# Attention and two gated MLPs on one core: eight weight units split earlier, high halves on VectorE, small operations on GpSimd

## The chip, the cores and the metric

The kernel runs on one core of one Trainium2 chip. Times are microseconds (us) of device time for one execution. The engines are called by the profile's names: PE is TensorE's matmul stream and PEld its weight loads, DVE is VectorE, ACT is ScalarE, POOL is GpSimd, and SP is SyncE, which here only issues DMAs.

## The reference

Attention of 4 batches with 12 heads over 448 tokens and 64 features, then two MLPs over the 1792 tokens. Cut to what matters:

```python
def rmsnorm(x, g):
    rms = np.sqrt(np.mean(x * x, axis=-1, keepdims=True) + 1e-06)
    return x / rms * g
q_n, k_n = (rmsnorm(q, g_q), rmsnorm(k, g_k))
scores = scale * np.matmul(q_n, k_n.transpose(0, 1, 3, 2))
scores = scores - np.max(scores, axis=-1, keepdims=True)
attn = np.exp(scores)
attn = attn / (np.sum(attn, axis=-1, keepdims=True) + 1e-09)
attn_out = np.matmul(attn, v)
x = attn_out.transpose(0, 2, 1, 3).reshape(B * S, H * D)      # 1792 x 768
x = (x @ w_a) * (x @ w_b) @ w_out                             # d_ff 1536, no activation
h = x @ w_in                                                  # d_ff 2048
g = np.maximum(h, 0.0) + alpha * np.minimum(h, 0.0)
out = g @ w_out2                                              # 1792 x 768
```

Queries, keys, values and norm weights are float32. The weight matrices of the MLPs are float64, so each value arrives as eight bytes.

## The kernel before

**Two programs in one.** The attention runs in steps (`att_steps`, 84 with work, each on two tiles of 128 query rows; a pair of heads has seven tiles): scores, softmax, transposition of the probabilities, product with the values. The 24 pairs of heads, six in a batch, follow each other. The six of batch 0 come first, in float32 with transposes on PE ("the first attention", up to 118 us). The others use float16 in two halves, high and low, and transposes by DMA. The MLPs run in 16 stages, `a0 y0 h0 o0 a1 y1 a2 h1 o1 y2 a3 h2 y3 o2 h3 o3`: the letter says which matrix is multiplied (a: `w_a` and `w_b`; y: `w_out`; h: `w2_in`; o: `w2_out`), the digit which batch. Attention steps of batches 1 to 3 are handed out among the ticks of a stage. `RATE` says how many a stage gets, and what is still missing before an a stage is run ahead of it.

**Weights.** Each matrix is read in units, 128x768 for a, y and h, 128x512 for o, 76 in all (a 24, y 12, h 16, o 24). The first time a unit is needed it is made on the chip, in four steps:

- `w_load`: SP's queue brings the float64 words, three buffers (`raw_p`).
- `w_convert`: ACT shifts the exponent of the upper words (L631), DVE shifts (L634) and joins the lower bits (L637) into a float32 tile. For o units DVE then multiplies by `inv_h`, the inverse scale of each of the rows' h units (L643). ACT sums the squares (L653).
- `w_scale`: PE sums over the partitions (`total`), and `power` makes from this a scale and its inverse, both powers of two.
- `w_split`: ACT writes the float16 high half (L686), DVE the low half (L687), and a DMA stores both in scratch memory (L690). The next batch reloads them from there, in `w_load`.

`advance(u)` drives these: while unit u is in use, loads run 10 units ahead, conversions 8, scales 6, splits 3. In the first attention it is called at every second step and reaches `u = -1`, which is what is ready when stage a0 begins. The products of PE take three matmuls for each tile (`prod`): high by high, high by low, low by high.

**Order.** A framework with a scheduler sets a fixed order of the instructions of each engine when the program is built, and waits are by semaphores. Each engine and each queue takes its instructions in that order.

**Small steps that the change touches.** `prep1` computes the inverse roots of the norms by three Newton rounds on a 128x30 tile on DVE, for two head pairs at a time; `prep2` multiplies queries and keys by them. `soft` takes the row maximum (DVE, L414), scales it by `esc` (ACT, L427, batches 1 to 3) and takes the exponential (ACT, L431) with its sum `su`. `probs_f` and `probs` add 1e-9 to `su` (DVE, L441 and L467) and take the reciprocal. In stage h the result of PE goes through ACT and DVE to a float32 tile, which is split by `cg` into `G` (L741, L742). In stage o each 128 columns are transposed back on PE and scaled by `cum` on DVE (L856) into `ob` for the output. The pool `slot` holds 35 tiles of 128x448 words for X, AB, Y and G.

Of the kernel before, what the change touches and what calls it, by code (L numbers as in the profile page):

```python
# [19 lines left out]
def attention_gated_mlps_kernel(  # L20
# [73 lines left out]
    icg = const.tile([128, 1], F32, name="icg")  # L94
    ssv = const.tile([KP, B, NP], F32, name="ssv")
# [14 lines left out]
    def power(total, s, i):  # L110
# [10 lines left out]
        nc.vector.tensor_scalar(i.bitcast(I32), h, 1.0, float(49 << 23), op0=ALU.mult, op1=ALU.add)  # L121
# [59 lines left out]
    def setup4():  # L181
# [10 lines left out]
        nc.vector.tensor_scalar(al, al, -1.0, 1.0, op0=ALU.mult, op1=ALU.add)  # L192
        nc.vector.tensor_scalar(icg, icg, 2.0 ** 31, None, op0=ALU.mult)
# [49 lines left out]
    def prep1(gs, c0=0, c1=NS):  # L243
# [166 lines left out]
    def soft(m):  # L410
# [15 lines left out]
        else:  # L426
            nc.scalar.activation(out=nm, in_=nm, func=AF.Copy, scale=esc)  # L427
# [33 lines left out]
    def probs(m):  # L461
# [5 lines left out]
        nc.vector.tensor_scalar(su, su, 1e-9, 2.0 ** -14, op0=ALU.add, op1=ALU.mult)  # L467
# [61 lines left out]
    state = dict(pin=True)  # L529
# [71 lines left out]

    def size(kind):
        return CHAINS[kind][2] * 128

    def w_load(u):
# [3 lines left out]
        if key in scratch:  # L609
            t = wh_p.tile([128, 2, 768], F16, tag="w16", name="w16")[:, :, 0:n]  # L610
            nc.sync.dma_start(out=t, in_=scratch[key])
            w16[u] = t
            return
# [7 lines left out]
    def w_convert(u):  # L621
# [18 lines left out]
        if kind == "o":  # L640
            k = CHAINS["o"][2]
            t3 = t.rearrange("p (k f) -> p k f", f=128)
            nc.vector.tensor_tensor(  # L643
                t3, t3,
                inv["h"][:, part * k:(part + 1) * k].unsqueeze(2).to_broadcast([128, k, 128]),
                op=ALU.mult,
            )
# [13 lines left out]
    def w_scale(u):  # L661
# [10 lines left out]
        for x in us:  # L672
            scales[x] = sc[:, (x - us[0]) // parts:(x - us[0]) // parts + 1]

# [5 lines left out]
    def w_split(u):  # L680
# [4 lines left out]
        w = wh_p.tile([128, 2, 768], F16, tag="w16", name="w16")[:, :, 0:n]  # L685
# [280 lines left out]
```

## Time and profile before

| what | value |
|---|---|
| median of 3 runs | 1285.5 us (1284.17 to 2438.65) |
| profiled execution, own time | 1286.1 us |
| span of the profiled execution | 1283.9 us |
| PE busy | 1177.9 us (92%) |
| PEld busy | 604.0 us (47%) |
| DVE busy | 709.6 us (55%) |
| ACT busy | 734.5 us (57%) |
| POOL busy | 9.8 us (1%) |
| mean granted clock of PE | 0.968 |
| moved by DMA | 234.66 MB, mean 183 GB/s |

A busy time is the time in which the engine had an instruction in work, over the whole span; weight loads overlap matmuls. The span runs from the first to the last recorded instruction, so 2.2 us of the execution's own time lie around it. The shares are means over stages that differ: the second half holds little but matmuls and reloads, the first half holds the attention and all the making of weights.

The stages begin, by their first matmul, at 118 (a0), 232 (y0), 295 (h0), 363 (o0) and 466 us (a1); y1 begins at 655 us.

### The profile page before, as it was taken

The page shows a single profiled execution, that of the slowest core. Times are in us where ns is not written, and L with a number is a line of the kernel's source. Part 1 is how long each engine was busy: PE and PEld are TensorE (multiplying, and loading weights), DVE is VectorE, ACT ScalarE, POOL GpSimd, SP SyncE. Part 2 cuts the span into 40 slices and gives each one's busy share as a digit, 9 for nine tenths or more (in the row PEclk, how much of TensorE's full clock was granted, in tenths as well). Part 3 has the DMA queues.
Part 4 walks back from the last instruction along what each step waited for, and adds up shares of the span by engine and source line. Part 5 has one row for each costly group of instructions (what it writes and reads, how often), then busy time and mean ns, then how long its engine had stood idle before and what let it go on. Part 6 is the DMA issues. An engine that isn't in the chain of part 4 may idle for free. (4 is left out here: it accounts for less than half of the span.)

```text
span 1283.9 us, 18197 instructions
## 1 busy us (share of the span) xinstructions
PE 1177.9 (92%) x6574; PEld 604.0 (47%) x6574; DVE 709.6 (55%) x1500; ACT 734.5 (57%) x1480; POOL 9.8 (1%) x32
## 2 busy tenths in 40 slices
PE   6897998888888889887999989999999999999998
PEld 3454544444443444443545545555555555555554
DVE  7988788879897857576545166443111351102410
ACT  7999898999886867577554256544222342212310
POOL 1000000000000000000000000000000000000000
PEclk9998998898998999997999999999999999999999
DMA  6548999999989899986865375687533333344343
GB/s 187 157 156 195 299 295 299 268 296 269 285 220 251 238 235 226 206 210 164 204 153 152 115 169 133 153 189 179 150 112 113 121 112 119 94 137 137 104 124 86
DMA packets 324489, 234.66 MB, mean 183 GB/s; under 512 B 190992, under 2 KB 297744, under 8 KB 324400
## 3 DMA queue, kind: packets, MB, share of 16 engines
q1 hardware_dynamic: 324288, 233.43, 68.9%
q8 instruction: 52, 0.85, 0.3%
q0 software_dynamic: 112, 0.07, 0.1%
q14 instruction: 37, 0.30, 0.1%
HBM read 155.79 MB, written 32.24 MB: 146 GB/s over the span
## 5 line engine op out<-in xcount | busy, mean ns | idle before, releaser
L108 PEld LDWEIGHTS <-w 128*128 128x128 f16 x4896 | 480.2, 100 | 488.8 <-issue 55.5
L108 PE MATMUL p<-x,w 128*128 128x448 f16 x1728 | 339.7, 356 | 10.1 <-ACT t L760 6.7
L108 PE MATMUL p<-g,w 128*128 128x448 f16 x1152 | 232.9, 359 | 9.9 <-DVE w L687 6.9
L108 PE MATMUL p<-y,w 128*128 128x448 f16 x1152 | 225.2, 357 | 0.0
L108 PE MATMUL p<-ab,w 128*128 128x448 f16 x864 | 170.8, 359 | 1.9 <-ACT ab L741 1.9
L108 PE MATMUL s<-kT,qT 128*64 128x448 f16 (+1 forms) x588 | 105.5, 408 | 32.4 <-ACT pf L431 24.7
L414 DVE TENSOR_REDUCE nm<-s 128x2 f32<-128x896 f32 x84 | 91.0, 1084 | 36.2 <-PE s L108 35.9
L475 DVE SCALAR_TENSOR_TENSOR p<-pf,ri,p 128x448 f16<-128x448 f32 x126 | 83.2, 680 | 37.9 <-ACT p L474 37.9
L474 ACT ACTIVATE p<-pf,ri 128x448 f16<-128x448 f32 x126 | 79.9, 662 | 31.9 <-DMA pT<-p 23.5
L431 ACT ACTIVATE pf<-s,nm,esc 128x448 f32<-128x448 f32 x126 | 90.2, 720 | 2.9 <-DVE p L475 1.5
L763 DVE SCALAR_TENSOR_TENSOR ab<-p,inv_a,t 128x448 f32<-128x448 f32 x48 | 32.6, 679 | 100.2 <-PE p L108 99.8
L847 ACT ACTIVATE t<-p,inv_o 128x448 f32<-128x448 f32 x24 | 25.6, 1066 | 102.2 <-PE p L108 102.2
L631 ACT ACTIVATE wf<-raw 128x768 f32<-128x768 f32 (+1 forms) x76 | 63.2, 835 | 28.7 <-DMA raw<-in_moe_w_out_dram 8.8
L856 DVE TENSOR_SCALAR ob<-p,cum 112x512 f32<-112x512 f32 x24 | 18.0, 749 | 107.1 <-PE p L854 56.8
L687 DVE SCALAR_TENSOR_TENSOR w<-wf,sc,w 128x768 f16<-128x768 f32 (+1 forms) x76 | 69.8, 927 | 4.0 <-ACT w L686 3.7
L766 ACT ACTIVATE junk<-ab 128x448 bf16<-128x448 f32 x48 | 27.5, 573 | 74.9 <-DVE ab L763 74.1
L833 DVE SCALAR_TENSOR_TENSOR t<-t,al,p 128x448 f32<-128x448 f32 x64 | 43.4, 679 | 47.6 <-ACT t L832 47.6
L637 DVE SCALAR_TENSOR_TENSOR wf<-raw,wf 128x768 int32<-128x768 int32 (+1 forms) x76 | 65.8, 868 | 0.4
L832 ACT ACTIVATE t<-p 128x448 f32<-128x448 f32 x64 | 34.6, 541 | 54.3 <-PE p L108 54.1
L686 ACT ACTIVATE w<-wf,sc 128x768 f16<-128x768 f32 (+1 forms) x76 | 64.5, 862 | 0.3 <-DVE sc L118 0.3
L653 ACT ACTIVATE junk<-wf 128x768 bf16<-128x768 f32 (+1 forms) x76 | 59.0, 776 | 8.5 <-DVE wf L643 2.9
L741 ACT ACTIVATE g<-t,cg 128x448 f16<-128x448 f32 x64 | 42.6, 666 | 34.7 <-DVE t L833 34.6
(131 smaller groups left out, 1003.3 us busy)
## 6 DMA issues: line engine op xcount, KB each, us to landing
w<-sc_a SPq DMA_DIRECT2D x72, 384.0 KB, 3.2
w<-sc_h SPq DMA_DIRECT2D x48, 384.0 KB, 3.1
w<-sc_o SPq DMA_DIRECT2D x72, 256.0 KB, 3.1
w<-sc_y SPq DMA_DIRECT2D x36, 384.0 KB, 3.2
raw<-in_moe_w_in_dram SPq DMA_DIRECT2D x16, 768.0 KB, 7.0
raw<-in_moe_w_out_dram SPq DMA_DIRECT2D x24, 512.0 KB, 5.0
raw<-in_moe_w_a_dram SPq DMA_DIRECT2D x12, 768.0 KB, 7.2
raw<-in_moe_w_b_dram SPq DMA_DIRECT2D x12, 768.0 KB, 6.0
```

Source lines behind the costliest of these rows:

```text
L108: nc.tensor.matmul(out=o, lhsT=a, rhs=b, start=first, stop=last)
L414: nc.vector.tensor_reduce(out=nm, in_=ps[:, :, 0:S], axis=AX.X, op=ALU.max, negate=True)
L431: nc.scalar.activation(out=pf, in_=ps[:, j, 0:S], func=AF.Exp, bias=nm[:, j:j + 1], scale=scale[j], accum_out=su[:, j:j + 1],)
L474: nc.scalar.activation(out=t[:, 0, :, 0:KP], in_=pf, func=AF.Copy, scale=r)
L475: nc.vector.scalar_tensor_tensor(out=t[:, 1, :, 0:KP], in0=pf, scalar=r, in1=t[:, 0, :, 0:KP], op0=ALU.mult, op1=ALU.subtract,)
L631: nc.scalar.activation(out=t, in_=hi.bitcast(F32), func=AF.Prelu, scale=2.0 ** -112, alpha=-(2.0 ** 32))
L637: nc.vector.scalar_tensor_tensor(out=ti, in0=lo, scalar=29, in1=ti, op0=ALU.logical_shift_right, op1=ALU.bitwise_or)
L653: nc.scalar.activation(out=junk(768, size(kind)), in_=t, func=AF.Square, accum_out=sums[0][:, j:j + 1])
L686: nc.scalar.activation(out=w[:, 0], in_=t, func=AF.Copy, scale=s)
L687: nc.vector.scalar_tensor_tensor(out=w[:, 1], in0=t, scalar=s, in1=w[:, 0], op0=ALU.mult, op1=ALU.subtract)
L741: nc.scalar.activation(out=x[:, 0], in_=t, func=AF.Copy, scale=s)
L833: nc.vector.scalar_tensor_tensor(out=t, in0=t, scalar=al[:, f:f + 1], in1=ps, op0=ALU.mult, op1=ALU.add)
```

## The change

**Units.** `EARLY` = 8 units get their halves in 16 tiles of the `slot` pool, and `advance` may run up to unit `LEAD` = 5 in the first attention, at three calls in four steps; in a0 it waits until the unit in use passes 5. For odd units the high half is made by DVE, for even ones by ACT as before. The scratch write is two DMAs instead of one.

**inv_h.** The multiplication of the o units by `inv_h` is taken out. `h_scales` folds it into the scale of `G` (`cgf`), once the last h unit has its scale. Until then stage h0 keeps `G` tiles as float32 in slots, and splits two in each later tick.

**Small operations.** To POOL go: the inverse power of two in `power`, the Newton rounds (from pair 3 on, four operations a round where there were three), the scaling of the maximum by `esc`, the addition to `su`, and two operations of the setup. `ob` goes from DVE to ACT. `RATE` gives a0 six attention steps for four, and o0 six for eight.

```diff
@@ power @@
-        nc.vector.tensor_scalar(i.bitcast(I32), h, 1.0, float(49 << 23), op0=ALU.mult, op1=ALU.add)
+        nc.gpsimd.tensor_scalar(i.bitcast(I32), h, 1.0, float(49 << 23), op0=ALU.mult, op1=ALU.add)
...
+        eng = nc.vector if gs[0] < 3 else nc.gpsimd
         for _ in range(3):
-            nc.vector.tensor_tensor(t, r, r, op=ALU.mult)
-            nc.vector.scalar_tensor_tensor(
-                out=t, in0=t, scalar=-0.5, in1=m, op0=ALU.mult, op1=ALU.mult
-            )
-            nc.vector.scalar_tensor_tensor(
-                out=r, in0=t, scalar=1.5, in1=r, op0=ALU.add, op1=ALU.mult
-            )
+            eng.tensor_tensor(t, r, r, op=ALU.mult)
+            eng.tensor_tensor(t, t, m, op=ALU.mult)
+            eng.tensor_scalar(t, t, -0.5, 1.5, op0=ALU.mult, op1=ALU.add)
+            eng.tensor_tensor(r, r, t, op=ALU.mult)
...
-            nc.scalar.activation(out=nm, in_=nm, func=AF.Copy, scale=esc)
+            nc.gpsimd.tensor_scalar(nm, nm, esc, 1.0, op0=ALU.mult, op1=ALU.mult)
...
-        nc.vector.tensor_scalar(su, su, 1e-9, None, op0=ALU.add)
+        nc.gpsimd.tensor_scalar(su, su, 1e-9, 1.0, op0=ALU.add, op1=ALU.mult)
...
+    EARLY, LEAD = 8, 5
+    early_w = [[slot(f"w{u}_{l}") for l in range(2)] for u in range(EARLY)]
...
-        if kind == "o":
-            k = CHAINS["o"][2]
-            t3 = t.rearrange("p (k f) -> p k f", f=128)
-            nc.vector.tensor_tensor(
...
+        if (kind, n) == ("h", KF2 - 1):
+            h_scales()
+
+    def h_scales():
+
+        mx = sm_p.tile([128, 1], F32, tag="mh", name="mh")
+        ci = sm_p.tile([128, 1], F32, tag="mh", name="ci")
+        nc.vector.tensor_reduce(out=mx, in_=inv["h"], axis=AX.X, op=ALU.max)
+        nc.vector.tensor_scalar(
+            ci.bitcast(I32), mx.bitcast(I32), -1.0, float(254 << 23), op0=ALU.mult, op1=ALU.add
+        )
+        nc.vector.tensor_scalar(cgf, inv["h"], ci, cg, op0=ALU.mult, op1=ALU.mult)
+        nc.gpsimd.tensor_tensor(icg, icg, mx, op=ALU.mult)
+        state["cgf"] = True
...
-        nc.scalar.activation(out=w[:, 0], in_=t, func=AF.Copy, scale=s)
+        if u < EARLY:
+            w = [x.rearrange("p l s -> p (l s)")[:, 0:n] for x in early_w[u]]
...
+        if u % 2:
+            nc.vector.tensor_scalar(w[0], t, s, None, op0=ALU.mult)
+        else:
+            nc.scalar.activation(out=w[0], in_=t, func=AF.Copy, scale=s)
...
-        nc.sync.dma_start(out=scratch[stream[u]], in_=w)
+        for l in range(2):
+            nc.sync.dma_start(out=scratch[stream[u]][:, l], in_=w[l])
...
-        advance(u)
+        advance(max(u, LEAD))
...
-            G[b, f] = split(t, cg, f"g{b}_{f}")
+            if state["cgf"]:
+                for x in sorted({f, min(raw)}):
+                    one(x)
+        for x in sorted(raw):
+            one(x)
...
-            nc.vector.tensor_scalar(ob, po, cum[:PT, b:b + 1], None, op0=ALU.mult)
+            nc.scalar.activation(out=ob, in_=po, func=AF.Copy, scale=cum[:PT, b:b + 1])
...
-    RATE = {"a0": 4, "y0": 5, "h0": 4, "o0": 8, "a1": 14, "y1": 7, "a2": 4, "h1": 4, "o1": 8, "y2": 6}
+    RATE = {"a0": 6, "y0": 5, "h0": 4, "o0": 6, "a1": 14, "y1": 7, "a2": 4, "h1": 4, "o1": 8, "y2": 6}
...
-        W0, EVERY = 4, 2
+        W0 = 3
...
-            if n >= W0 and (n - W0) % EVERY == 0:
-                advance((n - W0) // EVERY - 9 if n < 22 else -1)
+            if n >= W0:
+                advance(min((n - W0) * 3 // 4 - 9, LEAD))
```

In the order of ACT, at the first head pair's output in the first attention, there stood before (`wf<-raw` is the first step of a conversion, `junk` the sum of squares, `pf` an exponential, `pT<-p` and `kT` copies of transposes, `x<-x,sx` that output):

```order
L431 ACTIVATE pf,su<-s,nm,r 128x448 x2
L368 ACTIVATE sq,ssv<-vn 112x512
L631 ACTIVATE wf<-raw 128x768 x2
L459 COPY pT<-p 112x4x128
L523 ACTIVATE x_0_560<-x,sx 128x448
L368 ACTIVATE sq,ssv<-vn 112x512
L322 COPY kT_107<-p 128x448
L459 COPY pT<-p 112x4x128 x2
L431 ACTIVATE pf,su<-s,nm,r 128x448 x2
L653 ACTIVATE junk,ss<-wf 128x768
```

In the changed program the same engine has, around the same output:

```order
L633 ACTIVATE wf<-raw 128x768
L430 ACTIVATE pf,su<-s,nm,r 128x448 x2
L367 ACTIVATE sq,ssv<-vn 112x512
L647 ACTIVATE junk,ss<-wf 128x768
L458 COPY pT<-p 112x4x128
L522 ACTIVATE x_0_599<-x,sx 128x448
L633 ACTIVATE wf<-raw 128x768 x2
L367 ACTIVATE sq,ssv<-vn 112x512
L647 ACTIVATE junk,ss<-wf 128x768
L633 ACTIVATE wf<-raw 128x768
L321 COPY kT_107<-p 128x448
```

Conversions stand closer together: by the end of the first attention ACT has 15 for 11 and 14 sums of squares for 9, and DVE has 9 low halves for 5 and 4 high halves where it had none.

At the start of stage o0, DVE had before (`wf` are o units in conversion, `w` their halves, `g` a split of stage h):

```order
L634 TENSOR_SCALAR wf<-wf 128x512
L687 SCALAR_TENSOR_TENSOR w_4155<-wf,sc,w_4155 128x512
L637 SCALAR_TENSOR_TENSOR wf<-raw,wf 128x512
L833 SCALAR_TENSOR_TENSOR t<-t,al,p 128x448
L643 TENSOR_TENSOR wf<-wf,inv_h 128x512
L634 TENSOR_SCALAR wf<-wf 128x512
L742 SCALAR_TENSOR_TENSOR g_15_4162<-t,cg,g_15_4162 128x448
L637 SCALAR_TENSOR_TENSOR wf<-raw,wf 128x512
L687 SCALAR_TENSOR_TENSOR w_4189<-wf,sc,w_4189 128x512
L643 TENSOR_TENSOR wf<-wf,inv_h 128x512
```

In the changed program DVE has in that stage, after the start value of a Newton chain (`r<-t`, L260):

```order
L699 TENSOR_SCALAR w_4442<-wf,sc 128x512
L260 TENSOR_SCALAR r<-t 128x30
L382 SCALAR_TENSOR_TENSOR v_4491<-vr,sx,v_4491 112x8x64
L702 SCALAR_TENSOR_TENSOR w_4416<-wf,sc,w_4416 128x512
L702 SCALAR_TENSOR_TENSOR w_4442<-wf,sc,w_4442 128x512
L327 TENSOR_TENSOR qr<-qr,r 128x448
L636 TENSOR_SCALAR wf<-wf 128x512
L330 TENSOR_TENSOR qr<-qr,gbc 128x448
L639 SCALAR_TENSOR_TENSOR wf<-raw,wf 128x512
```

The products with `inv_h` are gone, a high half (L699) has come, and the user of the chain's result (`qr<-qr,r`) stands three instructions behind its start value, while the rounds between the two stand on POOL.

On POOL the program before has, from the end of the setup on (`cum` is the output's scale, first computed at the end of stage y0):

```order
L160 DMA gbc<-in_g_q_dram 128x64
L151 TENSOR_SCALAR gT<-gT 128x1
L161 DMA gkb<-in_g_k_dram 128x64
L162 DMA al<-in_moe_alpha_dram 128x16x1
L813 TENSOR_TENSOR cum<-ix,iab 128x1
L814 TENSOR_TENSOR cum<-cum,iy 128x1
```

In the changed program POOL has inside the first attention, among others (`su` feeds the reciprocal of a softmax, `inv_a` the a units' inverse scales, `t` and `r` are a Newton round):

```order
L440 TENSOR_SCALAR su<-su 128x2 x2
L122 TENSOR_SCALAR inv_a<-pw 128x2
L440 TENSOR_SCALAR su<-su 128x2
L122 TENSOR_SCALAR inv_a<-pw 128x2
L263 TENSOR_TENSOR t<-r 128x30
L264 TENSOR_TENSOR t<-t,m 128x30
L265 TENSOR_SCALAR t<-t 128x30
L266 TENSOR_TENSOR r<-r,t 128x30
```

Between the setup and the first `cum` POOL had nothing; now a whole Newton chain of twelve operations stands between two `su`. Over the program POOL has 30 Newton rounds in ten chains, 84 `su`, 63 `nm` and 45 inverse powers.

## Rows read from the trace of the kernel before

**Rows 1.** Busy time of each engine by stage; last: clock, DMA share, GB/s.

```profile
0.00:118.00 118.00, 91.56 (x554) 53.48 (x555) 99.52 (x302) 104.04 (x230) 5.68 (x16) 0.94 0.62 167
118.00:226.00 108.00, 99.06 (x543) 49.90 (x542) 89.95 (x176) 95.33 (x187) 0.00 (x0) 0.97 1.05 292
226.00:295.00 69.00, 55.85 (x308) 28.20 (x308) 58.59 (x122) 63.84 (x123) 1.79 (x4) 0.90 1.06 279
295.00:363.00 68.00, 63.54 (x342) 32.28 (x341) 62.34 (x125) 57.93 (x110) 0.00 (x0) 0.95 0.97 276
363.00:466.00 103.00, 84.50 (x465) 39.61 (x463) 89.30 (x197) 80.70 (x173) 0.00 (x0) 0.93 0.92 236
466.00:598.00 132.00, 111.35 (x665) 54.48 (x664) 84.58 (x180) 83.22 (x189) 0.19 (x1) 0.95 0.91 212
...
655.00:1284.00 629.00, 617.82 (x3398) 319.17 (x3396) 189.32 (x326) 211.02 (x396) 2.10 (x11) 0.99 0.49 131
```

**Rows 2.** The same view, two stretches inside the first attention.

```profile
32.00:64.00 32.00, 26.48 (x176) 15.46 (x173) 29.57 (x100) 31.86 (x73) 0.00 (x0) 0.98 0.56 157
64.00:96.00 32.00, 29.62 (x183) 16.65 (x181) 26.03 (x63) 29.63 (x67) 0.00 (x0) 0.96 0.50 156
```

**Rows 3.** Waits of PE: us in total, times, longest us.

```profile
PE s L108 <- ACT pf L431: 24.7, 12, 4.8
...
PE p L108 <- DVE w L687: 6.9, 5, 2.2
```

**Rows 4.** Groups of ACT from 0 to 118 us: busy us, mean ns.

```profile
L631 ACT ACTIVATE wf<-raw 128x768 f32<-128x768 f32 x9 | 8.4, 945 | 0.0
L653 ACT ACTIVATE junk<-wf 128x768 bf16<-128x768 f32 x9 | 7.9, 878 | 0.0
```

**Rows 5.** Groups of DVE by shape, whole span.

```profile
L687 DVE SCALAR_TENSOR_TENSOR w<-wf,sc,w 128x768 f16<-128x768 f32 x52 | 52.2, 1011 | 3.7 <-ACT w L686 3.7
L637 DVE SCALAR_TENSOR_TENSOR wf<-raw,wf 128x768 int32<-128x768 int32 x52 | 49.5, 954 | 0.4
...
L634 DVE TENSOR_SCALAR wf<-wf 128x768 int32<-128x768 int32 x52 | 28.8, 556 | 23.2 <-ACT wf L631 22.8
...
L634 DVE TENSOR_SCALAR wf<-wf 128x512 int32<-128x512 int32 x24 | 10.1, 421 | 4.5 <-ACT wf L631 4.2
L262 DVE SCALAR_TENSOR_TENSOR t<-t,m 128x30 f32<-128x30 f32 x33 | 6.2, 188 | 0.6
...
L441 DVE TENSOR_SCALAR su<-su 128x2 f32<-128x2 f32 x21 | 3.4, 163 | 3.3 <-ACT pf L431 3.2
```

**Rows 6.** Groups of ACT by shape, whole span.

```profile
L686 ACT ACTIVATE w<-wf,sc 128x768 f16<-128x768 f32 x52 | 48.0, 932 | 0.0
...
L427 ACT ACTIVATE nm<-nm,esc 128x2 f32<-128x2 f32 x63 | 18.4, 292 | 46.9 <-DVE nm L414 46.9
L686 ACT ACTIVATE w<-wf,sc 128x512 f16<-128x512 f32 x24 | 16.5, 710 | 0.3 <-DVE sc L118 0.3
```

**Rows 7.** Groups of DVE from 363 to 466 us.

```profile
L643 DVE TENSOR_TENSOR wf<-wf,inv_h 128x512 f32<-128x512 f32 x18 | 12.2, 683 | 0.0
...
L856 DVE TENSOR_SCALAR ob<-p,cum 112x512 f32<-112x512 f32 x5 | 3.7, 746 | 0.1
```

**Rows 8.** Timeline of POOL: start us, us, instruction [idle before].

```profile
230.47 0.95 POOL L813 TENSOR_TENSOR cum<-ix,iab 128x1 f32<-128x1 f32 x1 [221.20 <-DVE pw L115]
...
293.55 0.19 POOL L815 TENSOR_TENSOR cum<-cum,icg 128x1 f32<-128x1 f32 x1
293.82 0.19 POOL L816 TENSOR_TENSOR cum<-cum,ix 128x1 f32<-128x1 f32 x1
```

**Rows 9.** Timeline of DVE beside the first of them.

```profile
230.36 1.01 DVE L687 SCALAR_TENSOR_TENSOR w<-wf,sc,w 128x768 f16<-128x768 f32 x1
```

**Rows 10.** DMA issues from 466 to 598 us: count, KB each, us to landing.

```profile
w<-sc_a SPq DMA_DIRECT2D x21, 384.0 KB, 4.6
...
pT<-p SPq DMA_TRANSPOSE x32, 3.5
```

More of the change, by code (lines that the diff above doesn't have):

```diff
@@ L94, in attention_gated_mlps_kernel @@
     icg = const.tile([128, 1], F32, name="icg")
+    cgf = const.tile([128, KF2], F32, name="cgf")
     ssv = const.tile([KP, B, NP], F32, name="ssv")
@@ L191, in setup4 @@
         nc.vector.tensor_scalar(cg, cg, 2.0 ** -31, None, op0=ALU.mult)
-        nc.vector.tensor_scalar(al, al, -1.0, 1.0, op0=ALU.mult, op1=ALU.add)
-        nc.vector.tensor_scalar(icg, icg, 2.0 ** 31, None, op0=ALU.mult)
+        nc.gpsimd.tensor_scalar(al, al, -1.0, 1.0, op0=ALU.mult, op1=ALU.add)
+        nc.gpsimd.tensor_scalar(icg, icg, 2.0 ** 31, None, op0=ALU.mult)
     P = [dict() for _ in range(B * NP)]
@@ L527, in pv_out @@
         P[g] = None
-    state = dict(pin=True)
+    state = dict(pin=True, cgf=False)
     preps = (prep2, prep3, prep4)
@@ L611, in w_load @@
             nc.sync.dma_start(out=t, in_=scratch[key])
-            w16[u] = t
+            w16[u] = [t[:, l] for l in range(2)]
             return
@@ L684, in w_split @@
         n = t.shape[1]
-        w = wh_p.tile([128, 2, 768], F16, tag="w16", name="w16")[:, :, 0:n]
-        nc.scalar.activation(out=w[:, 0], in_=t, func=AF.Copy, scale=s)
+        if u < EARLY:
+            w = [x.rearrange("p l s -> p (l s)")[:, 0:n] for x in early_w[u]]
+        else:
+            w = wh_p.tile([128, 2, 768], F16, tag="w16", name="w16")[:, :, 0:n]
+            w = [w[:, l] for l in range(2)]
+        if u % 2:
+            nc.vector.tensor_scalar(w[0], t, s, None, op0=ALU.mult)
+        else:
+            nc.scalar.activation(out=w[0], in_=t, func=AF.Copy, scale=s)
         nc.vector.scalar_tensor_tensor(
-            out=w[:, 1], in0=t, scalar=s, in1=w[:, 0], op0=ALU.mult, op1=ALU.subtract
+            out=w[1], in0=t, scalar=s, in1=w[0], op0=ALU.mult, op1=ALU.subtract
         )
-        nc.sync.dma_start(out=scratch[stream[u]], in_=w)
+        for l in range(2):
+            nc.sync.dma_start(out=scratch[stream[u]][:, l], in_=w[l])
         w16[u] = w
@@ L723, in unit @@
     def unit():
-        w = w16[cur[0]]
-        return w.rearrange("p l (k f) -> p l k f", f=128)
+        return [x.rearrange("p (k f) -> p k f", f=128) for x in w16[cur[0]]]
     def prod(o, w, kk, x, first, last):
-        hi, lo = w[:, 0, kk, :], w[:, 1, kk, :]
+        hi, lo = w[0][:, kk, :], w[1][:, kk, :]
         mm(o, hi, x[:, 0], first, False)
@@ L823, in stage_h, with one @@
     def stage_h(b):
+        raw = {}
+        def one(f):
+            t = raw.pop(f)
+            G[b, f] = x = slot(f"g{b}_{f}")
+            nc.scalar.activation(out=x[:, 0], in_=t, func=AF.Copy, scale=cgf[:, f:f + 1])
+            nc.vector.scalar_tensor_tensor(
+                out=x[:, 1], in0=t, scalar=cgf[:, f:f + 1], in1=x[:, 0],
+                op0=ALU.mult, op1=ALU.subtract,
+            )
         for f in range(KF2):
@@ L830, in stage_h @@
             next_w()
-            t = tmp()
+            raw[f] = t = tmp() if state["cgf"] else slot32(f"g32_{b}_{f}")
             nc.scalar.activation(out=t, in_=ps, func=AF.Relu, scale=-1.0)
@@ L860, in finish @@
             )
+        c = cum[:, b:b + 1]
+        nc.gpsimd.tensor_tensor(c, ix[:, b:b + 1], iab[:, b:b + 1], op=ALU.mult)
+        nc.gpsimd.tensor_tensor(c, c, iy[:, b:b + 1], op=ALU.mult)
+        nc.gpsimd.tensor_tensor(c, c, icg, op=ALU.mult)
+        nc.gpsimd.tensor_tensor(c, c, ix[:, b:b + 1], op=ALU.mult)
         late = None
@@ L915, in attention_gated_mlps_kernel @@
         state["pin"] = False
-        advance(-1)
+        advance(LEAD)
         def step():
```

11 lines of the change are left out of this document (1 added, 10 removed).

## The prediction, made before the changed kernel had run

> **What bounds the kernel now.** I read the stages first, because the shares over the whole span mix two halves that differ. In the view of busy time by stage [rows 1] the reader should subtract PE's busy time from each stretch: after 655 us PE works 617.8 of 629 us, and nothing that relieves another engine can save more than the 11 us left there. PE's idle time lies in front: 26.4 us in the first attention, 8.9 in a0, 13.2 in y0, 4.5 in h0, 18.5 in o0 and 20.7 in a1. These 92 us are what the change can win or enlarge. The work of PE is the same in both programs, so each term below is a change of PE's idle time, and the two attention steps that move from o0 to a0 count for nothing in the sum by themselves.
>
> Who is late differs by stage. In the first attention DVE and ACT are both close to full: from 32 to 64 us ACT works 31.9 of 32 us, and from 64 to 96 us it has 2.4 us free [rows 2], while the DMA share there is 0.56 and 0.50. In the waits of PE [rows 3] the largest single entry is the scores' matmul waiting for the exponential, 24.7 us in 12 waits. From a0 to o0 the picture turns: the DMA share is 1.05, 1.06, 0.97 and 0.92 [rows 1], while ACT and DVE each have 7 to 22% free. These stages load float64 weights, write halves, transpose and reload at once. In o0 both DVE (89.3 of 103 us) and the queues are candidates. PE waits there are few and long, the product's wait for a low half on DVE taking 6.9 us in 5 [rows 3].
>
> **The change part by part.**
>
> First attention, four more conversions and earlier splits. ACT gets 4 x 0.945 for conversions and 5 x 0.878 for sums of squares [rows 4], and loses two `nm` of 0.29 [rows 6]: +7.6 us. DVE gets 4 x (0.556 + 0.954) for shifts and joins, 4 x 1.011 for low halves [rows 5] and four new high halves. The high half on DVE is not in this trace; the shift of one float32 tile (0.556) and the two-input join (0.954) bound it, and I take 0.56, since it also has one input and a constant. DVE loses 21 additions of 0.163 and two Newton chains of nine operations at 0.188 [rows 5], and pays some 2 us for the fourth operation in the rounds that stay. Its sum is 6.0 + 4.0 + 2.2 - 3.4 - 3.4 + 2.2 = +7.6 us. With ACT at 31.9 of 32 this lands on the path, at least in the middle. All of it could fit the 14.5 us that ACT has free over the 118 us [rows 1], or POOL's chains could come on top: a dependent operation there starts 0.27 us after the one before [rows 8], so a chain of twelve takes 3.2 us, and two chains bring it to 14. Bounds 0 and +14; **I take +7**, as the fullest stretches lie where the conversions go.
>
> a0. ACT loses twelve high halves of 0.932 [rows 6] and three conversions, gets two attention steps and `nm` no more: 6 us less in sum. DVE gets high halves and steps, 3 us more. DMA: about 4.5 units' raw loads and writes move into the first attention, where the share is 0.62. A unit is 0.77 MB in and 0.38 MB out, at 292 GB/s [rows 1] 3.9 us, so 17.6 us leave. The two more steps bring about 10.4 us of transfers (an estimate: in the stretch from 466 to 598 us the DMA share of 0.91 is 120 us of work; 21 reloads of 384 KB [rows 10] and a few smaller ones at 292 GB/s are about 36 of them, which leaves some 84 for the 32 transposes of 16 steps). Net -7 us on the fullest resource. Of 8.9 us idle this can close all or nothing, and DVE's 3 us can come on top: -9 to +4. **I take -3**, a third of the idle time, since DVE at 83% and ACT at 88% are not what is fullest.
>
> y0. ACT loses seven high halves [rows 6], 6.5 us, DVE gets six at 0.56. The queues stay at 1.06 [rows 1], and what a0 leaves undone arrives here. Idle 13.2; -8 to +2, **taken -4**.
>
> h0. The same exchange with six units, seven products with `inv_h` less, against nine tiles split later in pairs. Idle is 4.5 only: -4.5 to +2, **taken -2**.
>
> o0. Here DVE loses 17 products of 0.683 and six `ob` of 0.746 [rows 7], 11.6 + 4.5, and two steps' work; it gets 11 high halves, which a 512-wide shift prices at 0.42 [rows 5], 4.6 us. ACT loses eleven at 0.71 [rows 6] and gets six `ob`. In sum DVE goes from 89 to about 67 of 103 us and the queues lose 10 us of transposes. I expect o0 to look like h0, which has 4.5 us idle: 18.5 - 4.5 = **-14**. If only the DVE waits close, -7; if all, -18.5.
>
> a1 has 20.7 us idle with DVE and ACT at 64%; it waits for the steps of the attention, whose chain loses one operation on ACT and gains two hops to POOL. -5 to +5, **taken 0**. After 655 us `ob` on ACT lies beside PE at 98% [rows 1], at no cost; were that cover gone, it would be 18 times 0.75. The second half of each scratch write has time until the next batch's reload, hundreds of us later, and the tile behind it is free only with it; splits run three units ahead, 13 us in a0, against 4.6 us for a transfer to land [rows 10]. I set it to nothing.
>
> POOL's waits. In-order DVE now waits inside the chain of the norms: before, the nine Newton operations were its own, 1.7 us; now it has one to five instructions to do until POOL has its 3.2 us. That is 1 to 3 us per chain, covered by other idle time where DVE is below 90%. Behind the waiting product stand low halves of weights, on which PE waits [rows 3]; I count it inside the ranges.
>
> There is evidence against cheap POOL operations. At 230.47 POOL began a 128x1 product that took 0.95 us in place of 0.19 [rows 8], and DVE was in a two-input operation from 230.36 to 231.37 [rows 9]; the one ended just after the other. The Trainium skill, "SBUF — State Buffer", section Terms, says that VectorE and GpSimd share a port pair under an exclusive lock and that the loser blocks for the whole instruction; the trace has this one case that agrees. By that rule every small operation here may wait up to one DVE instruction, and the sum would be that of the second rival below; by the 0.19 us of most such rows it stays as it is.
>
> Sum: +7 - 3 - 4 - 2 - 14 + 0 = -16. Against the profiled execution's own 1286.1 us (0.6 above the median of 1285.5): **1270 us**. It is not likely that all bounds on one side are reached at once; about a third of their spread gives the forecast by itself 1258 to 1284.
>
> **The rivals.**
>
> Relief goes further. If DVE and ACT, not the queues, are what is late in a0 to o0, idle time there falls by 40 of its 45 us while the first attention pays 7: 1286 - 33 = **1253**. For it: the waits of PE name ACT and DVE, not DMA [rows 3]. Against it: DMA shares around one [rows 1].
>
> POOL is late (slower). Softmax steps go through POOL twice, `nm` and `su`. If each addition to `su` waits 0.95 - 0.19 = 0.76 us as in [rows 8], and half of the 84 lie on the path, that is 32 us; five of the ten Newton chains at 3 us give 15. -16 + 47 = +31: **1317**. It decides from 0.16 us for each of these 102 operations on, where the gain of 16 is used up. For it: 52 of 76 low halves are two-input DVE operations of 1.0 us [rows 5], and DVE is full of such. Against it: the softmax is pipelined a step ahead.
>
> Work only moves. If the queues bound a0 to h0 and the two extra steps eat the relief, these three terms are zero, o0 closes half (-7) and the first attention takes it back (+7): **1286**.
>
> **How the numbers follow.** Forecast 0.52, further relief 0.27, POOL late 0.09, only moved 0.12. The range 1247 to 1290 takes in the forecast, the third rival and most of the first; left out are the second (0.09) and about 0.08 at the far ends. A change of 2%, 25.7 us, is about what a measurement of this kernel can tell from none. Faster than 1259.8: the first rival and a little of the forecast's lower end, less the first's upper end, 0.28. Slower than 1311.2: most of the second, 0.08. Within: 0.64.
>
> **What would show it.** In the profile after, a first attention some 7 us longer with ACT near full in its middle; o0 with about 5 us of PE idle, a0 and y0 still near 6 and 9 with a DMA share near one. The first rival shows as a0 to o0 at 95% PE and more. The second shows as POOL rows for `su` and `nm` well above 0.2 us and as ACT or DVE waiting for them. The third shows as y0 and o0 unchanged. What would make me wrong is a chain that I priced as beside the path: DVE waiting for Newton on POOL with weight halves queued behind it, or the slots taken by the eight units making X or AB wait in a0.

## The result: slower by 1.2%

The changed kernel takes 1302.2 us (median of 4 runs, 1299.33 to 1304.75), the kernel before 1286.6 beside it: 1.0123, 95% interval 1.01 to 1.0146. One of the four executions of the kernel before took 2438.65 us, and the ratio leaves it out. The forecast was 1270 with a range to 1290.

The busy time of each engine by stage, of the kernel after, cut at its own stage edges (columns as in [rows 1]; the seventh line is the stretch behind y1, which runs from 615 to 672 us here and ran from 598 to 654 us before):

```profile
0.00:135.30 135.30, 96.17 (x567) 55.62 (x568) 108.07 (x286) 112.08 (x242) 25.41 (x74) 0.92 0.64 184
135.30:252.50 117.20, 102.39 (x563) 51.84 (x562) 99.50 (x179) 92.36 (x187) 22.57 (x52) 0.94 1.00 276
252.50:321.50 69.00, 59.32 (x321) 29.25 (x321) 55.75 (x100) 55.59 (x105) 12.89 (x16) 0.89 0.98 251
321.50:384.50 63.00, 60.20 (x339) 31.45 (x339) 57.49 (x108) 49.19 (x97) 8.25 (x17) 1.00 1.03 281
384.50:475.80 91.30, 78.91 (x424) 37.50 (x425) 69.83 (x142) 65.14 (x135) 15.94 (x32) 0.93 0.92 232
475.80:615.20 139.40, 116.97 (x665) 56.12 (x664) 77.18 (x137) 80.09 (x174) 20.47 (x69) 0.90 0.88 201
...
672.10:1303.00 630.90, 619.62 (x3402) 319.79 (x3400) 170.59 (x277) 217.71 (x397) 16.37 (x64) 0.99 0.49 131
```

Against the stages of the kernel before by their first matmuls ([rows 1] cuts a0 from y0 at 226 us, but y0's first matmul stands at 232), the first attention grew by 17.7 us, a0 by 3, y0 by 6 and a1 by 7.5; h0 shrank by 5 and o0 by 12, of which two attention steps are part. Behind a1 only 2 us were added. PE's idle time rose from 106.0 to 116.0 us, and its busy time from 1177.9 to 1187.0 for the same matmuls, at a mean granted clock of 0.959 where it was 0.968. So in these two executions half of the loss is waiting and half a lower granted clock; in a1 the clock (0.90 for 0.95) has 5.6 of the 7.5 us, 116.97 us of busy time for 111.35. The changed kernel's other three executions had a mean clock of 0.962 to 0.964, and the medians lie 15.6 us apart where these two lie 18.7.

ACT and DVE lost work, as planned: 734.5 to 708.6 us and 709.6 to 671.7. What came instead is in two views of the kernel after. The groups of POOL by shape (busy us, mean ns, idle before and what ended it):

```profile
L426 POOL TENSOR_SCALAR nm<-nm,esc 128x2 f32<-128x2 f32 x63 | 42.2, 670 | 394.7 <-DVE nm L413 366.3 <-DVE pw L116 12.0 <-DVE tots L132 9.9
L466 POOL TENSOR_SCALAR su<-su 128x2 f32<-128x2 f32 x63 | 16.4, 260 | 132.5 <-ACT pf L430 132.3
L263 POOL TENSOR_TENSOR t<-r 128x30 f32<-128x30 f32 x30 | 9.7, 323 | 36.8 <-DVE r L260 35.1
...
L440 POOL TENSOR_SCALAR su<-su 128x2 f32<-128x2 f32 x21 | 8.2, 390 | 73.2 <-ACT pf L430 72.8
```

The waits, as in [rows 3] but of ACT, DVE and PE for what moved:

```profile
ACT pf L430 <- POOL nm L426: 86.2, 49, 4.9
...
DVE ri L467 <- POOL su L466: 75.6, 40, 3.5
...
DVE qr L327 <- POOL r L266: 25.0, 9, 3.9
...
PE s L109 <- ACT pf L430: 23.4, 13, 7.9
```

In the kernel before, these waits stood in the place of the first two:

```profile
ACT nm L427 <- DVE nm L414: 46.9, 34, 4.2
...
DVE su L467 <- ACT pf L431: 47.8, 32, 1.9
```

The scaling `nm` took 0.67 us in the mean where ACT took 0.29 [rows 6], and ACT, which had waited 47 us for the maxima, now waits 86 us for the scaled ones. PE's own wait for exponentials did not grow with it, 23.4 us for 24.7 [rows 3]: its added idle time is spread over many rows, the largest growth being that of the first attention's transposes behind DVE's `pf`, from 2.3 to 10.8 us. How `nm` comes to be late, two moments of the kernel after show, in the timeline (start us, us, instruction, idle before). First the softmax step at 507 us:

```profile
506.22 1.08 DVE L413 TENSOR_REDUCE nm<-s 128x2 f32<-128x896 f32 x1
...
507.22 0.68 DVE L352 TENSOR_TENSOR k<-kr,k 112x512 f16<-112x512 f32 x1
507.41 1.16 POOL L426 TENSOR_SCALAR nm<-nm,esc 128x2 f32<-128x2 f32 x1 [2.90 <-DVE nm L413]
507.82 0.62 DVE L349 TENSOR_TENSOR q<-qr,q 128x448 f16<-128x448 f32 x1
508.36 0.68 DVE L778 SCALAR_TENSOR_TENSOR ab<-p,inv_a,t 128x448 f32<-128x448 f32 x1
508.61 0.72 ACT L430 ACTIVATE pf<-s,nm,esc 128x448 f32<-128x448 f32 x1 [1.29 <-POOL nm L426]
```

DVE goes on to two products of two on-chip tiles, the second of which ends at 508.44; POOL's operation on 256 numbers, begun at 507.41, ends at 508.57, just behind it. ACT's exponential starts 0.04 us later, so the hop to another engine is short. In the step of 510.67 us it spans three such products and takes 1.82 us. Where DVE was idle, reduced a tile (from the accumulators or on the chip) or worked on one or two columns it takes 0.26 to 0.27, in 32 of the 63. The other 31 took over 0.3 us, and each ends 0.05 or 0.13 us behind the end of a DVE instruction on wider on-chip tiles. Then the step at 571 us:

```profile
571.00 1.08 DVE L413 TENSOR_REDUCE nm<-s 128x2 f32<-128x896 f32 x1
...
574.70 0.25 POOL L266 TENSOR_TENSOR r<-r,t 128x30 f32<-128x30 f32 x1
574.93 0.73 POOL L426 TENSOR_SCALAR nm<-nm,esc 128x2 f32<-128x2 f32 x1
574.98 0.62 DVE L327 TENSOR_TENSOR qr<-qr,r 128x448 f32<-128x448 f32 x1 [2.89 <-POOL r L266]
...
575.69 0.72 ACT L430 ACTIVATE pf<-s,nm,esc 128x448 f32<-128x448 f32 x1 [3.97 <-POOL nm L426]
```

The maximum is ready at 572.08, but on POOL a Newton chain is in front, and `nm` ends at 575.66. DVE sat idle for 2.9 us for the chain's result, ACT 4.0 us for `nm`. This is the rarer case: only two of the 63 `nm` had a Newton chain in front, and began 2.8 and 2.4 us behind their maximum; 60 began within 0.2 us of it.

### The profile page after: what moved, and what is told of

It reads as the page before. It is cut to its first block, busy times and chain, and to the rows that moved or that the text cites. A ratio compares the mean times of both kernels' runs of the same rounds, so it can differ in the third digit from the quotient of the medians.

```text
span 1303.0 us, 18359 instructions
## 1 busy us (share of the span) xinstructions
PE 1187.0 (91%) x6574; PEld 608.0 (47%) x6574; DVE 671.7 (52%) x1284; ACT 708.6 (54%) x1403; POOL 128.3 (10%) x347
## 4 chain that ended last, share of the span: by engine, by line
PE 56%; DVE 13%; DMA 12%; ACT 9%; issue 5%; POOL 3%; SPq 2%; ACTq 0%; DVEq 0%; POOLq 0%
PE p L109 50%; DMA raw<-in_moe_w_out_dram 3%; ACT pf L430 2%; PE x L109 2%; PE s L109 2%; DVE nm L413 2%; DMA raw<-in_moe_w_in_dram 2%; DVE wf L639 2%; DVE w L702 1%; DVE p L474 1%; DMA pT<-p 1%; DMA kr<-in_k_dram 1%; POOL nm L426 1%; ACT junk L647 1%; DMA sc_o<-w 1%
## 5 line engine op out<-in xcount | busy, mean ns | idle before, releaser
L109 PE MATMUL s<-kT,qT 128*64 128x448 f16 (+1 forms) x588 | 106.9, 411 | 29.3 <-ACT pf L430 23.4
L473 ACT ACTIVATE p<-pf,ri 128x448 f16<-128x448 f32 x126 | 81.1, 662 | 34.4 <-DMA pT<-p 24.7
L854 DVE SCALAR_TENSOR_TENSOR t<-t,al,p 128x448 f32<-128x448 f32 x55 | 37.3, 679 | 97.1 <-ACT t L853 97.0
L426 POOL TENSOR_SCALAR nm<-nm,esc 128x2 f32<-128x2 f32 x63 | 42.2, 670 | 394.7 <-DVE nm L413 366.3
L109 PE MATMUL x<-pT,v 112*64 112x448 f16 x432 | 48.5, 373 | 8.9 <-DVE pw L116 6.6
L853 ACT ACTIVATE t<-p 128x448 f32<-128x448 f32 x55 | 29.6, 538 | 49.2 <-PE p L109 49.2
L839 ACT ACTIVATE g<-t,cgf 128x448 f16<-128x448 f32 x55 | 36.7, 667 | 35.6 <-DVE t L854 35.6
```

What stands on the lines that cost most here:

```text
L109: nc.tensor.matmul(out=o, lhsT=a, rhs=b, start=first, stop=last)
L426: nc.gpsimd.tensor_scalar(nm, nm, esc, 1.0, op0=ALU.mult, op1=ALU.mult)
L473: nc.scalar.activation(out=t[:, 0, :, 0:KP], in_=pf, func=AF.Copy, scale=r)
L839: nc.scalar.activation(out=x[:, 0], in_=t, func=AF.Copy, scale=cgf[:, f:f + 1])
L854: nc.vector.scalar_tensor_tensor(out=t, in0=t, scalar=al[:, f:f + 1], in1=ps, op0=ALU.mult, op1=ALU.add)
```

## The experiments

Two theories stood after the result. P: the small operations on POOL are on the path. E: the earlier units overfill ACT and DVE in the first attention. Each edit is against the changed kernel unless it says otherwise, and ratios are to the kernel before. "Off POOL" means that every small operation is back on its old engine.

**All off POOL.**

```diff
-            nc.gpsimd.tensor_scalar(nm, nm, esc, 1.0, op0=ALU.mult, op1=ALU.mult)
+            nc.scalar.activation(out=nm, in_=nm, func=AF.Copy, scale=esc)
...
-        eng = nc.vector if gs[0] < 3 else nc.gpsimd
...
-        nc.gpsimd.tensor_scalar(i.bitcast(I32), h, 1.0, float(49 << 23), op0=ALU.mult, op1=ALU.add)
+        nc.vector.tensor_scalar(i.bitcast(I32), h, 1.0, float(49 << 23), op0=ALU.mult, op1=ALU.add)
```

> The changed kernel with every small operation back where it was (the scaling of the maximum on ACT, the addition to su, the Newton rounds of three operations and the inverse powers on DVE); the early units, the folded inv_h, the high halves on DVE, ob on ACT and RATE stay changed. Theory P (POOL late): the small operations on POOL cost the 17 us that the first attention and the 7.5 us that the stretch of a1 grew by; then the first attention falls from 135 to about 125 us, a1's stretch from 139 to about 132, and the time is 1275 to 1283. Theory E (the early conversions overfill ACT and DVE in the first attention): the first attention stays at 131 to 135 us, and the time is 1294 to 1300.

1283.4 us, 0.9982 (0.9965 to 0.9999): as P said, at the end of its range. Windows of this kernel, first attention and a1:

```profile
0.00:129.20 129.20, 97.66 (x559) 57.29 (x559) 109.22 (x322) 112.00 (x244) 5.67 (x16) 0.91 0.66 192
...
464.70:596.40 131.70, 113.11 (x665) 55.02 (x663) 83.58 (x179) 83.78 (x190) 0.19 (x1) 0.94 0.95 213
```

Of the 19 us, 7.7 return in a1's stretch, at 131.7 for 131.9 before, 6 in the first attention (some 3 of them not by this edit, as the run with only `nm` back shows) and 4 in y0. But the first attention stays 11 us above the 118 of before: a part of E is true there.

**The old schedule of units.**

```diff
-    EARLY, LEAD = 8, 5
+    EARLY, LEAD = 0, -1
...
-                advance(min((n - W0) * 3 // 4 - 9, LEAD))
+                advance((n - W0) // EVERY - 9 if n < 22 else -1)
```

> The changed kernel with the old schedule of units in the first attention: no unit in slots, a call at every second step, up to the unit before the first; all else stays changed. Theory P: POOL's operations still delay the softmax chain, so the first attention falls by no more than 6 us, to 129 or more, a0 gets longer by as much, and the time is 1298 to 1306. Theory E: the first attention is back at 118 to 122 us, and the time is 1284 to 1290.

1302.1 us, 1.0131 (1.01 to 1.0162). The first attention falls from 135 to 123 us, more than P had expected, and a0 takes it all back, 117 to 128. The early units only move work here.

**Only the small operations, in the kernel before.** The first edit turned round, in the old kernel.

> The kernel before with only the small operations moved to POOL. Theory P: the first attention grows by 8 to 12 us, a1's stretch by 7, a0 and y0 by some 5 together, and the time is 1302 to 1312. Theory E: POOL's operations are beside the path, 1283 to 1290.

1302.4 us, 1.0132 (1.0089 to 1.0176): the whole loss of the change, from this part alone. The two windows that grew are the first attention and a1:

```profile
0.00:122.50 122.50, 94.42 (x553) 55.06 (x554) 96.00 (x263) 102.83 (x227) 19.60 (x70) 0.92 0.55 154
474.70:613.60 138.90, 114.90 (x665) 56.09 (x664) 77.67 (x138) 79.53 (x173) 20.61 (x69) 0.93 0.90 201
```

They are 5 and 7 us longer than before, though DVE has 3 and 7 us less to do [rows 1]; o0 grew by 4.

**Both undone: off POOL, and the old schedule of units.** The first two edits together.

> The changed kernel with both undone, the small operations and the early schedule; what stays is the folded inv_h, the high halves of odd units on DVE, ob on ACT and RATE. If theory P and theory E each hold a part, the gain of h0 and o0 seen in the changed kernel (17 us, of which some 10 are the two attention steps moved to a0) stands alone: 1272 to 1280, with a first attention at 118. If the gain in o0 rested on the early units, 1284 to 1290.

1281.8 us, 0.9971 (0.9952 to 0.9989). Less than expected: h0 and o0 gave 14 us, but a0 and y0, with two steps more, took 10. With and without early units is the same once POOL is out (1283 and 1282).

**Only `nm` back on ACT.** The first two lines of the first diff.

> The changed kernel with only the scaling of the maximum by esc back on ACT; the additions to su, the Newton rounds and the inverse powers stay on POOL. Theory N (this one operation carries most of what POOL costs behind the first attention, since it stands between each maximum and its exponential, and takes 0.67 us on POOL in the mean for 0.29 on ACT): the stretch of a1 falls from 139 to 132 to 134 us, the first attention stays at 133 to 136, the time is 1289 to 1294. Theory R (the wait is shared out over all the operations, or lies in the Newton chains): a1 falls by less than 3 us, the time is 1297 to 1302.

1288.0 us, 1.0021 (1.0004 to 1.0038). Fourteen of the 19 us come back by one operation, and ACT's wait is back at 47 us (from the waits, then a1's stretch):

```profile
ACT nm L426 <- DVE nm L413: 47.3, 40, 4.6
...
464.60:600.10 135.50, 113.27 (x665) 55.24 (x664) 77.07 (x136) 84.46 (x190) 12.88 (x53) 0.93 0.89 206
```

Theory N by the time, though not by the stretches: a1 is 135.5, of which PE is idle 22.2 us, as in the changed kernel (22.4), and what returns there is clock, 0.93 for 0.90. The first attention is 130 for 135, and that is not `nm`: the two programs give every engine the same instructions up to the first `nm` at 131 us. The two executions part at 32 us (the changed kernel's first, then this one's):

```profile
32.00:36.00 4.00, 4.00 (x25) 2.48 (x26) 2.88 (x7) 3.27 (x9) 0.19 (x1) 0.59 0.88 232
...
32.00:36.00 4.00, 4.00 (x44) 2.50 (x44) 3.79 (x10) 3.96 (x10) 0.19 (x1) 1.00 1.01 277
```

In the changed kernel's execution PE had been idle for 2.2 us just before, in the other for 0.95, and from there the first is some 3 us late. So a stretch of one execution can be off by 3 us with the same instructions; the 14 us are of medians, over 4 and 10 executions.

**Only the Newton rounds back on DVE.**

> The changed kernel with only the Newton rounds back on DVE, three operations a round; the scaling of the maximum, the additions to su and the inverse powers stay on POOL. DVE waited 25 us in 9 waits for POOL's chains in the changed kernel. Theory R: these waits are on the path, the first attention falls by 3 us or more and the time is 1290 to 1296. Theory N: they are covered by other waits, the time is 1298 to 1303.

1293.8 us, 1.0053 (1.0028 to 1.0077). Eight us, as R said, with the first attention 8 us shorter at 127, some 3 of which can be the changed kernel's execution. Theories N and R are both true; that 14 and 8 add to 22 and not to 19 is no more than two orders can differ by (below).

**`nm` and Newton back; `su`, the inverse powers and the setup stay on POOL.**

> The changed kernel with the scaling of the maximum back on ACT and the Newton rounds back on DVE; the additions to su, the inverse powers and the setup stay on POOL. One edit alone gave 14 us back, the other 8, all together 19. Theory N+R (these two are the price, and the rest on POOL lies beside the path): 1281 to 1286. If the additions to su have a price of their own between the exponential and the reciprocal, 1288 to 1293.

1282.0 us, 0.9966 (0.9944 to 0.9989). These two are the whole price, as far as these runs can tell. Beside the run before this one, `nm` gives 12 us back with no Newton chain on POOL at all, and beside the run with `nm` back, the Newton rounds give 6. Yet the view of waits of this kernel still has this row:

```profile
DVE ri L469 <- POOL su L468: 62.4, 35, 2.3
```

DVE waits 62 us for `su`, on which POOL spends 0.367 us in the mean, where DVE spent 0.163 on the like one of the first attention [rows 5]. That costs nothing that shows. It is 15 us more than DVE waited in the kernel before for the sum itself (47.8), where ACT's wait for `nm` grew by 39: the smaller growth lies beside the path, the other on it.

**`nm` on POOL in the kernel before, nothing else.**

> The kernel before with one edit, the scaling of the maximum by esc on POOL (63 instructions). Theory N: it waits there for the end of DVE's operation with operands in the on-chip memory, 0.67 us in the mean in the changed kernel, and alone on POOL has nothing queued in front of it, so the price is less than the 14 us that its return gave the changed kernel: a1's stretch 134 to 137 us (132 before), the time 1290 to 1297. Theory R (it cost 14 us in the changed kernel only because Newton chains stood in front of it on POOL): 1283 to 1288.

1291.7 us, 1.0045 (1.0026 to 1.0065), with a1 at 134.2, both within what N said. With an otherwise nearly empty POOL `nm` still takes 0.60 us in the mean, ACT waits 27 us more for it than for the maximum before, and the time is 6 us longer:

```profile
ACT pf L431 <- POOL nm L427: 73.4, 40, 4.7
```

That fits a price of the wait for DVE's instructions by itself, but 6 us is at the edge of what the order alone can do. Theory R doesn't explain the rest of the 14: only two `nm` of the changed kernel had a chain in front, and without chains on POOL the return of `nm` still gave 12 us. There `nm` took 0.78 us in the mean and ACT waited 40 us more than with it on ACT:

```profile
ACT pf L432 <- POOL nm L428: 87.8, 48, 5.5
```

So ACT's added wait and the price go together in these three cases (27 us and 6, 39 and 14, 40 and 12); why `nm` is held longer in the changed kernel was not tested.

**`nm` on DVE.** In the changed kernel off POOL, then in the kernel before, then off POOL with the old schedule:

```diff
-            nc.scalar.activation(out=nm, in_=nm, func=AF.Copy, scale=esc)
+            nc.vector.tensor_scalar(nm, nm, esc, None, op0=ALU.mult)
```

> The changed kernel with every small operation off POOL, and the scaling of the maximum by esc on DVE, right behind the maximum, where it needs no other engine. Theory N, carried on: the way from the maximum to the exponential is a chain whose length counts, so that 0.15 us on DVE for 0.29 us on ACT shortens a1's stretch by 2 to 4 us and the time is 1276 to 1281. If only the wait for the port on POOL counted and not the length of the chain, 1282 to 1286, as with the operation on ACT (1283).

> The kernel before with one edit, the scaling of the maximum by esc on DVE. Theory N with the length of the chain: a1's stretch 128 to 131 us, the time 1277 to 1282. If the gain of the same edit in the changed kernel (6 us) came only with the early units or the shared high halves: 1284 to 1288.

> The changed kernel with every small operation off POOL, the old schedule of units in the first attention, and the scaling of the maximum by esc on DVE. If the early units only move work, as the pair with and without them says (1283 and 1282), this is 1274 to 1279, beside 1277 with them; if they pay once the softmax chain is short, 1281 to 1285.

1277.4 us (0.9938, 0.9918 to 0.9957), 1288.2 us (1.0019, 0.9996 to 1.0042) and 1283.5 us (0.999, 0.9975 to 1.0005). The same edit gives 6 us, loses 3, loses 2. The idea that the chain from maximum to exponential should be as short as can be has no support; from the end of the reduction (L414) to the start of the exponential (L431) the median of 63 steps is 0.83 us with `nm` on DVE in the kernel before, and 0.48 with it on ACT. So on DVE the way was not shorter but longer, and with `nm` on POOL, alone or in the changed kernel, it is 0.76: its median length is not what costs.

**High halves back on ACT, off POOL.**

```diff
-        if u % 2:
-            nc.vector.tensor_scalar(w[0], t, s, None, op0=ALU.mult)
-        else:
-            nc.scalar.activation(out=w[0], in_=t, func=AF.Copy, scale=s)
+        nc.scalar.activation(out=w[0], in_=t, func=AF.Copy, scale=s)
```

> The changed kernel with every small operation off POOL and every high half on ACT again. Theory Q (from a0 to o0 the queues bound, so that which engine makes the high halves does not matter): 1281 to 1287, within 4 us of the kernel with the high halves shared (1283). Theory B (ACT's relief by some 25 us of high halves was a gain on the path of y0, h0 and o0): 1288 to 1294, with y0 to o0 longer by 5 us or more.

1281.8 us, 0.9962 (0.9943 to 0.9982), beside 1283.4. Who makes the high halves makes no difference that can be told.

**More transfers, meant for o0, off POOL.**

```diff
+        if stream[u][0] == "o" and u % 2:
+            more = hbm.tile([128, n], I64, name=f"more_{u}")
+            nc.sync.dma_start(out=more.rearrange("p (k f) -> p k f", f=128), in_=source(*stream[u]))
```

> The changed kernel with every small operation off POOL, and twelve more transfers of 512 KB, each of which copies the float64 words of an odd o unit from one place in the chip's main memory to another; nothing waits for them and they hold no buffer. They add 6.3 MB to the 21.5 MB that o0 moved in 90 us. Theory Q (o0 is bound by the transfers, DMA share 0.92): o0 grows from 90 to 105 to 115 us, the time is 1298 to 1308. Theory W (o0 waits for conversions on ACT and DVE or for the sums on PE, and the queues have room): o0 grows by less than 5 us, the time is 1284 to 1289.

1279.2 us, 0.9955 (0.9933 to 0.9977). It doesn't answer its question: since nothing precedes the copies, the scheduler placed all twelve between 7 and 53 us. Its window of the first attention:

```profile
0.00:132.20 132.20, 97.29 (x558) 57.69 (x559) 109.49 (x321) 108.98 (x239) 5.68 (x16) 0.90 0.76 232
```

That stretch grew by 3 us, and yet the whole is 4 us faster than without. Useless transfers can't be a gain; they changed the order of the rest. So differences of 3 to 6 us between two orders aren't to be read as the price of an edit.

**Writes that can't start early, off POOL.** Every o unit's scratch write is issued twice, the second to a place that nothing reads.

```diff
+        if stream[u][0] == "o":
+            again_ = hbm.tile([128, 2, n], F16, name=f"sd_{u}")
+            for l in range(2):
+                nc.sync.dma_start(out=again_[:, l], in_=w[l])
```

> The changed kernel with every small operation off POOL, and the scratch write of each o unit issued a second time, to a place that nothing reads: 6.3 MB more from the halves' own tiles, which cannot start before the unit is split and so lies in o0. Theory Q (the transfers bind o0): o0 grows from 90 us by 12 to 22 us, the time is 1295 to 1306. Theory W (o0 waits for conversions, splits and sums, and the queues have room beside them): o0 grows by less than 5 us, the time is 1281 to 1288.

1295.2 us, 1.0066 (1.0044 to 1.0088). The window of o0 in the kernel off POOL, without these writes:

```profile
374.70:464.70 90.00, 77.95 (x424) 37.69 (x425) 74.34 (x172) 70.15 (x148) 0.00 (x0) 0.92 0.92 239
```

The window of o0 in this kernel, with them:

```profile
372.00:475.70 103.70, 81.27 (x425) 39.13 (x426) 75.43 (x172) 71.36 (x149) 0.00 (x0) 0.88 0.96 264
```

The same instructions on ACT and DVE, within two, and o0 is 13.7 us longer: transfers in this stage are paid for, 10 us of it as idle time of PE and 3 as clock. The time and the growth are those of theory Q, but the rate rose from 239 to 264 GB/s, so the queues were not at their most before; the second writes also hold the units' tiles for longer, which this run doesn't separate.

**The old RATE, off POOL; and with the old schedule of units too.**

```diff
-    RATE = {"a0": 6, "y0": 5, "h0": 4, "o0": 6, "a1": 14, "y1": 7, "a2": 4, "h1": 4, "o1": 8, "y2": 6}
+    RATE = {"a0": 4, "y0": 5, "h0": 4, "o0": 8, "a1": 14, "y1": 7, "a2": 4, "h1": 4, "o1": 8, "y2": 6}
```

> The changed kernel with every small operation off POOL and the old RATE, four attention steps in a0 and eight in o0. Theory M (the two steps only move, with 5 us of PE's work and their transfers): a0 is shorter by 7 to 12 us, o0 longer by as much, the time is 1280 to 1288. If the move itself was a gain, because early units make room in a0: 1289 to 1295. If it was a loss: 1272 to 1279.

> The changed kernel with every small operation off POOL, the old schedule of units in the first attention, and the old RATE; what stays is the folded inv_h, the shared high halves and ob on ACT. If the moved steps cost 8 us whatever else is there: 1272 to 1276, and the early units are worth nothing. If the old RATE pays only beside early units, since these empty a0: 1279 to 1286.

1275.5 us (0.9904, 0.9869 to 0.994) and 1280.0 us (0.9956, 0.9937 to 0.9975). The first beats both kernels and is the fastest that ran. Its windows of a0 and o0:

```profile
127.00:237.00 110.00, 100.24 (x555) 51.50 (x553) 99.98 (x215) 89.06 (x182) 0.95 (x1) 0.97 1.00 284
363.60:456.20 92.60, 78.47 (x465) 38.56 (x466) 80.28 (x183) 77.27 (x166) 0.00 (x0) 0.98 1.00 254
```

a0 is 6.6 us shorter than with six steps, o0 only 2.6 longer. With the old schedule of units the old RATE gives 2 us (1281.8 to 1280.0), beside early units 8. That fits early units that empty a0, if the extra steps don't fill it again, but 4.6 us between the two kernels is what an accident of order can make, and the next run has the same edit beside early units again.

**The old RATE and `nm` on DVE, off POOL.**

> The changed kernel with every small operation off POOL, the old RATE, and the scaling of the maximum by esc on DVE. If the two edits that helped one by one (8 us and 6 us from 1283) add up: 1267 to 1271. If what the second gave was an accident of the order, as its loss of 3 us in the kernel before and of 2 us without early units suggests: 1273 to 1281.

1276.7 us, 0.993 (0.991 to 0.9951). They don't add up. Against the kernel with `nm` on DVE and the new RATE (1277.4) the old RATE gives 1 us, though a0 is again 6 us shorter and o0 4 longer: the same edit gave 8, 2 and 1 us.

## Why the prediction was wrong

**The step that failed is the price of POOL.** I set the waits for POOL at nothing beyond the ranges, "covered by other idle time where DVE is below 90%". Taking these operations off gives 18.7 us, and moving them alone into the kernel before costs 15.9. In profile it came as idle time and as a lower granted clock, and the sum, which went by idle time alone, had no term for the clock. The second rival named the place, and its evidence was the 0.95 us in [rows 8] that ended with DVE's product in [rows 9]; I gave it 0.09. That one row was the rule, not the exception: 31 of 63 `nm` were held up in the same way. The Trainium skill ("SBUF — State Buffer", Terms) says of the port pair that the two engines share that it is "Lock-allocated, exclusive, held for the full instruction". The ends of the 31 agree with it, and operations of up to 2.2 us show that the wait can last through several DVE instructions, more than the one that I read out of it.

**The rival had the wrong operation.** It priced 42 additions to `su` at 0.76 us and left `nm` out. Measured, `su` costs nothing that shows, and `nm` alone gives 12 to 14 us on its return: it stands between a maximum and its exponential, where ACT waits in order with all that is queued behind. I had written the argument against the rival, "the softmax is pipelined a step ahead", and it holds for the one and not the other. How ACT's wait reaches PE is only in part in the rows: PE's wait for exponentials is 23.4 us with `nm` on POOL and 19.1 with it on ACT. The rival's Newton term, 15 us, measured 6 to 8; a chain took 3.8 us (571.18 to 574.95) where I had put 3.2.

**The first attention, +7.** With POOL out, it is 10.9 us longer with early units than without (118.3 to 129.2), 7.0 of it idle time of PE and the rest a lower granted clock, 0.93 to 0.91. Two more executions with the same instructions in this stretch, those of the doubled writes and of the old RATE, took 126.2 and 127.0, and one more with the old schedule 117.0, so the term measures 8 to 12. It is right in kind, and the clock was not in it.

**a0 to o0, -23, and a1, 0.** With POOL out, PE's idle time against before changed by -1.1 in a0, -2.2 in y0, -0.7 in h0, -6.5 in o0 and -2.1 in a1. The first four are on the side that I forecast, a0 to h0 at a third to a half of the size, though changes of 1 or 2 us of one execution prove little. (By their first matmuls a0 had 12.9 and y0 9.2 us of idle time before; my 8.9 and 13.2 came from the cut at 226.) The largest error among these is o0, -14: I reasoned from DVE's relief, and DVE did go from 89 to 74 us of work there. But the DMA share stayed at 0.92, and the doubled writes show that more transfers are paid for in this stage. The third rival's "work only moves" is nearest for this part of the change: without POOL's operations it is worth 3 us.

**The steps that "count for nothing".** I had written that the sum needn't hold the two attention steps moved from o0 to a0, since PE's work is the same. Moving them back gave 8, 2 and 1 us in three pairs of kernels, so whether they have a price is not shown.

**What stays open.** What the folded `inv_h` and `ob` are worth by themselves was not run, nor how much of o0's growth under doubled writes is the queues and how much the tiles held. Why `nm` costs 12 to 14 us in the changed kernel and 6 in the kernel before, or whether part of that is order, is not known either. Whether 1275.5 against 1280.0 is the early units' gain or order can't be told from these runs.

## What to carry to other kernels

Before a small operation goes to an idle engine, ask who waits for its result and what its new engine waits for: 63 operations of 0.29 us, moved off ACT, here cost 12 to 14 us of the whole, while 84 others, for which DVE waited over 60 us in sum, cost nothing that shows. Read a wait beside what stood in its place before: of ACT's 86 us, 47 were there already. An in-order queue shared by a long chain and a short urgent step makes the step as late as the chain, but count how often, here twice in 63. And where a static scheduler reorders everything after each edit, an unrelated edit shows how much the order alone moves (4 us here, and one edit gained 6, lost 3 and lost 2); gains of that size are not gains yet.

## What the runs showed that I had not expected

POOL's `nm` ranged from 0.265 to 2.2 us with what DVE ran beside it, and DVE's one-input shift of a weight tile (L636) held it up too, to 0.64 us at 187.59 us, while a reduction of an on-chip tile (L242), which ran all through the one at 152.67 us, did not (0.27). The new high half of a 128x768 unit has this row in the groups of DVE by shape, of the kernel after:

```profile
L699 DVE TENSOR_SCALAR w<-wf,sc 128x768 f16<-128x768 f32 x26 | 15.9, 613 | 0.2 <-PE p L109 0.2
```

It took 0.613 us, near the 0.56 that the shift suggested, for 0.932 on ACT [rows 6]. And PE's granted clock took part in the loss: 9 us more busy time for the same matmuls in the profiled execution of the changed kernel, whose mean of 0.959 says that it ran more of the time at the lower of the two levels, 1.2 GHz for 2.4.
